# Thirty small loads on SyncE and six early stores on ScalarE in a decode kernel (1 core)

## The chip, the cores and the metric

The kernel runs on one core of a Trainium2 chip. Its metric is the device time of one execution in microseconds (us); smaller is better. A core has engines that run their own instruction streams side by side: TensorE (PE, matrix products), VectorE (DVE), ScalarE (ACT), GpSimd (POOL) and SyncE (SP), which here does nothing but issue transfers. They wait for one another through semaphores. Transfers between the chip's memory and the core's own memory are carried by 16 DMA engines; SyncE and ScalarE each issue into a queue of their own.

## The reference

One token for each of B = 2 batch rows goes through attention over a cache and through an MLP, and a gate mixes the two:

```
g = sigmoid((x * gate_w).sum(-1))                       # x: 2 x 1 x 1024
q = x @ wq                                              # 32 heads of 128
p = softmax(q . k_cache / sqrt(128))                    # k_cache: 2 x 32 x 16384 x 128, bf16
a = (p . v_cache) @ wo
x1 = x + shifted(gelu(layernorm(x) @ w1)) @ w2          # one position: the shifts leave zeros
b = x1 + gelu(layernorm(x1) @ w3) @ w4                  # F = 3584
out = g * a + (1 - g) * b                               # 2 x 1 x 1024, bf16
```

The two caches are 268 MB each and are read once. Everything else is small. Since the sequence has one position, the shifted input of the w2 product is zero, and the kernel does not load w1.

## The kernel before, in words

The kernel is first written down as a plan: `_Plan` holds for each engine a list of operations in order, each with its waits. `pl.add` appends an instruction, `pl.dma` appends a transfer on an engine's queue and returns the event "it has landed". The lists are then emitted engine by engine. An engine runs its list strictly in order: an operation whose wait isn't met holds up all that stand behind it.

Big loads go through a ring of five slots of 32 KB per partition. `queue_load` puts them into one list, in the order wq (two halves), w2, w3 (two halves), w4 (two halves), then for each of 32 pairs of heads the K load and the V load, and last wo (two halves, the second of them cut into five pieces). `pump` issues the head of that list on SyncE as soon as the plan has released its slots, with a wait for the release; `release` is called by the stage that has read a slot last. A K or V load fills two slots: 128 rows of 64 KB, 8.39 MB. K goes to slots 3 and 4 or 2 and 3 in turn (`k_slots`), V always to 0 and 1. So K of pair n+1 is issued when the first half of the scores of pair n is done, and V of pair n+1 when the value products of pair n are done. The names K0, K1, V3 and so on below count pairs from 0.

Ahead of the pairs stand the stages of `pro_stages`: the gate, the product with w2, the norm, the product with w3, the gelu (`gelu_stage`, whose tanh on ScalarE is L448 and whose result GT_bf on VectorE is L450), the product with w4 and the row bgrow (`st_bg`). ScalarE issues six small loads at the start: x and gate_w (L560, L561) and four pieces of x into `xrow` (L563), which `st_bg` adds.

For each pair n: `do_T` transposes K in place on VectorE (L647), `do_S` forms the scores on TensorE (L653), `do_softmax` takes the maximum, lets ScalarE do the exponential (L674) and transposes its result, `do_PV` multiplies with V on TensorE (L689), and `do_out` copies the sums on ScalarE (L698) and stores the two heads' column on VectorE (L703). The pairs are a hardware loop on TensorE, VectorE and ScalarE, two pairs to a turn; SyncE's list is unrolled. At the end `do_aproj` multiplies with wo (L726), VectorE copies the result (L750), and SyncE and ScalarE store one batch row each (L752).

Of the kernel before, what the change touches and what calls it, by code (L numbers as in the profile page):

```python
# [9 lines left out]
BF16 = mybir.dt.bfloat16  # L10
# [110 lines left out]
def build_kernel(nc, A_x, A_k, A_v, A_wq, A_wo, B_w1, B_w2, B_w3, B_w4, gate_w, out, dbg=None):  # L121
    dbg = dbg or {}
    B, Sq, D = A_x.shape
# [4 lines left out]
    P = 128  # L128
# [32 lines left out]
    PR = 32 * (NQ - 1) + 2  # L161
    assert DQ <= 512

    with ExitStack() as st:
        block = st.enter_context(nc.Block())
        sb = lambda name, shape, dt: st.enter_context(nc.sbuf_tensor(name, shape, dt))
# [34 lines left out]
        xrow = sb("xrow", [P, DQ], BF16)  # L201
        bgrow = sb("bgrow", [P, DQ], F32)
        orow = sb("orow", [P, DQ], BF16)
        m24 = sb("m24", [P, 2, NQ], F32)
        m2 = sb("m2", [P, 2], F32)
        gm = sb("gm", [P, 2], F32)
# [16 lines left out]
        sem = lambda n: st.enter_context(nc.semaphore(n))  # L223
        esems = {e: sem("e_" + e) for e in ENGS}
        s_ring = [sem(f"dr{i}") for i in range(NRS)]
        s_misc = sem("dmisc")
        s_gw = sem("dgw")
        s_out = [sem(f"dout{i}") for i in range(2)]
        s_xr = sem("dxr")
        s_tail = [sem(f"dtl{i}") for i in range(len(wo_runs[1]))]  # L230
        pl = _Plan(esems)
# [38 lines left out]
        for hp in range(HP):  # L270
# [7 lines left out]
                    waits=(ev_rowm,), sig=True)  # L278
# [3 lines left out]
        ev_cab = pl.add("dve", lambda e: e.tensor_scalar(cAB[:, 1:2], rowv[:, :], -NEG_BIG, NEG_BIG, op0=ALU.mult, op1=ALU.add),  # L282
                        waits=(e0,), sig=True)

        dma_q = []
        dma_done = {}
        slot_of = {}
# [12 lines left out]
        def pump():  # L300
            while dma_q and all(i in slot_free for i in dma_q[0][2]):
                key, fns, slots = dma_q.pop(0)
                waits = sum((slot_free.pop(i) for i in slots), ())
                slot_of[key] = slots[0]
                slots_of[key] = slots
                for k, fn in enumerate(fns):
                    dsem = s_ring[slots[0]] if len(fns) == 1 else s_tail[k]
                    dma_done[key] = dma_done[key, k] = pl.dma("sp", (lambda e, fn=fn, idx=slots[0]: fn(e, idx)), dsem,
                                                              waits=waits if k == 0 else ())

        def release(key, ev, slots=None):
            for idx in slots or slots_of[key]:
                assert idx not in slot_free
                slot_free[idx] = tuple(ev) if isinstance(ev, (tuple, list)) else (ev,)
            pump()
# [51 lines left out]
        evd = {}  # L367
# [176 lines left out]
        key = ("w2", 0)  # L544
        put([row_stage(key, list(range(NBD)), 0, NBD, lambda kc: shT_bf[:, kc, :], "const", last=True), hs_columns], key)
        put([st_x1, ln_a(x1T_f[:, :, :], "x1", st2_ps, "xn2"), ln_b(st2_ps, "xn2", None)])
        for hi in range(2):
            key = ("w3", hi)
# [3 lines left out]
        for hi in range(2):  # L552
            key = ("w4", hi)
# [8 lines left out]
        for qd in range(NQ):  # L562
            ev_xr = pl.dma("act", lambda e, qd=qd: e.dma_start(xrow[32 * qd:32 * qd + 2, :], A_x[:, 0, qd * DQ:(qd + 1) * DQ]), s_xr,  # L563
                           waits=(ev_xr0,))
# [8 lines left out]
        for pi in range(2):  # L573
            queue_load(("wo", pi), wloads[("wo", pi)], ((4, 3)[pi],))
        pump()

        def xcols(row, b_n, nb):
# [4 lines left out]
        for nb in range(NBD):  # L582
            last = pl.add("pe", lambda e, nb=nb: e.transpose(tr_ps[:, nb * 4:nb * 4 + 3], xcols(xg_row, 3, nb), ident[0:3, 0:3]),
                          waits=(ev_x, ev_gw, ev_ident), sig=(nb == NBD - 1))
# [10 lines left out]
        for hi in range(2):  # L595
            key = ("wq", hi)
            ev_arr = arrived(key)
            wv = ring_w(slot_of[key], RQ, HD)
            for r in range(RQ):
                kc = hi * RQ + r  # L600
                for h in range(H):
                    lastmm = (h == H - 1)
                    def fn(e, h=h, r=r, kc=kc, wv=wv, first=first):
                        return e.matmul(q_ps[:, h, :], lhsT=wv[:, r, h * Dh:(h + 1) * Dh], rhs=xT_bf[:, kc, :],  # L604
                                        start=first, stop=(kc == NBD - 1), skip_group_check=True)
# [6 lines left out]
        for bp in range(NBP):  # L612
            evp = pl.add("pe", lambda e, bp=bp: e.matmul(q4_ps[:, bp, :], lhsT=PermQ[:, bp, :],
                                                        rhs=q_sb[:, :, :].rearrange("p h b -> p (h b)"), start=True, stop=True),
                         waits=(ev_q, ev_const, ev_r0), sig=(bp == NBP - 1))
# [15 lines left out]
        def do_Z(n):  # L631
            g0 = (n // B * HP) * B + n % B
            for hp in range(HP):
                ev = pl.add("pool", lambda e, hp=hp: e.tensor_tensor(  # L634
                    Z[:, :, ZO:ZO + P].rearrange("p t (i c) -> p t i c", c=32)[:, :, 2 * hp:2 * hp + 2, hp],
                    q4_f[:, :, g0 + hp * B:g0 + hp * B + 1].broadcast_to([P, NBP, 2]),
                    mask4[:, 2 * hp:2 * hp + 2].unsqueeze(1).broadcast_to([P, NBP, 2]), op=ALU.mult),
                    waits=(ev_q4, ev_const, ev_S.get(n - 1)), sig=(hp == HP - 1))
            return ev
# [5 lines left out]
        def do_T(n, u):  # L645
            ap = chunk(n, u, TC).bitcast(F32)
            return pl.add("dve", lambda e: e.transpose(ap, ap), waits=(arrived(("k", n)),), sig=True)  # L647

        def do_S(n, u, w, first, last):
            kv = chunk(n, u, 1).rearrange("p (j b k t) -> p j b k t", j=JU, b=2, k=32)  # L650
            end = u % UH == UH - 1
            for bp in range(NBP):
                ev = pl.add("pe", lambda e, bp=bp: e.matmul(  # L653
                    S_ps[:, 0:NCOL], lhsT=Z[:, bp, ZO - 2 * u:ZO - 2 * u + P], rhs=kv[:, :, bp // 2, :, bp % 2],
                    start=(first and bp == 0), stop=(last and bp == NBP - 1), skip_group_check=True),
                    waits=w, sig=(end and bp == NBP - 1))
                w = ()
            if end:
                ev_S[n] = ev
                release(("k", n), ev, (slots_of["k", n][u // UH],))  # L660
# [22 lines left out]
        def do_PV(n, ev_pt):  # L683
            s0 = slot_of[("v", n)]
            vv = ring[:, s0:s0 + 2, :].rearrange("p s (u j d) -> p (s u) j d", u=UH, j=JU)
            w = (ev_pt, arrived(("v", n)))
            for jj in range(JU):
                for cg in range(4):
                    ev = pl.add("pe", lambda e, jj=jj, cg=cg: e.matmul(  # L689
                        acc_ps[32 * cg:32 * cg + 32, 0:512], lhsT=PT_sb[:, 32 * jj:32 * jj + 32], rhs=vv[:, 4 * cg:4 * cg + 4, jj, :],  # L690
                        start=(jj == 0), stop=(jj == JU - 1), tile_position=(0, 32 * cg), skip_group_check=True), waits=w,
                        sig=(jj == JU - 1 and cg == 3))
                    w = ()
            release(("v", n), ev)
            return ev

        def do_out(n, ev_pv, ev_rc):
            e1 = pl.add("act", lambda e: e.activation(acc_sb[:, :], acc_ps[:, 0:512], ACT.Copy), waits=(ev_pv,), sig=True)  # L698
            for w in range(4):
                e2 = pl.add("pe", lambda e, w=w: e.matmul(oT_ps, lhsT=acc_sb[:, w * P:(w + 1) * P], rhs=dsel[:, w, :],  # L700
                                                          start=(w == 0), stop=(w == 3)), waits=(e1,) if w == 0 else (), sig=(w == 3))
            b = n % B
            return pl.add("dve", lambda e, i: e.scalar_tensor_tensor(  # L703
                OT_sb[:, bass.ds(i * B * HP + b * HP, HP)], oT_ps, gT[:, b:b + 1], recip[:, :], op0=ALU.mult, op1=ALU.mult),
                waits=(e2, ev_rc), sig=True, dyn=True)
# [26 lines left out]

        for run in pro_stages:
            run()
        for n in range(NPR):
            pl.mark[n] = {e: len(pl.ops[e]) for e in ENGS}
            ev_z = do_Z(n)
            us = [h * UH + v for h in k_order[n % 2] for v in range(UH)]
            for k in range(0, NU, TC):
                ev_t = do_T(n, us[k])  # L740
                for t in range(TC):
                    w = () if t else (ev_t,) if k else (ev_t, ev_z) + pro_ev
                    do_S(n, us[k + t], w, k + t == 0, k + t == NU - 1)
            ev_pt, ev_rc = do_softmax(n)
            ev_OT = do_out(n, do_PV(n, ev_pt), ev_rc)
# [2 lines left out]

        ev_alast = do_aproj()
        ev_fin = pl.add("dve", lambda e: e.tensor_copy(orow[0:PR, :], rows_ps[0:PR, 0:DQ]), waits=(ev_alast,), sig=True)  # L750
        for b, eng in enumerate(("sp", "act")):
            ev_out = pl.dma(eng, lambda e, b=b: e.dma_start(out[b, 0, :].rearrange("(q n) -> q n", q=NQ), orow[b:PR:32, :]), s_out[b],  # L752
                            waits=(ev_fin,))
            pl.add(eng, lambda e, ev=ev_out: e.wait_ge(ev.sem, ev.val))
# [27 lines left out]
def bass_gated_mix__mha_block_cached__mixer_s_mlp__decode_kernel(  # L782
    nc: bass.Bass,
    A_x: bass.AP,
    A_k_cache: bass.AP,
    A_v_cache: bass.AP,
    A_wq: bass.AP,
    A_wo: bass.AP,
    B_x: bass.AP,
    B_w1: bass.AP,  # L790
    B_w2: bass.AP,
    B_w3: bass.AP,
    B_w4: bass.AP,
    gate_w: bass.AP,
    out: bass.AP,
):
    build_kernel(nc, A_x, A_k_cache, A_v_cache, A_wq, A_wo, B_w1, B_w2, B_w3, B_w4, gate_w, out)
# [28 lines left out]
```

## Time and profile before

| What | Value |
|---|---|
| time, median of 3 runs | 1326.04 us (1326.04 to 1326.1) |
| the profiled execution's own time | 1325.93 us |
| its span, first to last instruction | 1324.1 us |
| mean granted TensorE clock | 0.789 |
| read from memory | 570.44 MB, 431 GB/s over the span |
| TensorE busy | 785.1 us (59%) |
| VectorE busy | 657.2 us (50%) |
| ScalarE busy | 45.7 us (3%) |

How to read it: times in the traces are us from the start of the span, single durations of instructions often ns. L653 is line 653 of the kernel. In the order of time a row gives start, duration, engine, line, operation, what it writes and reads, and in brackets how long the engine idled before and what ended that. PE is the product, PEld the loading of its weights; SPq and ACTq are the transfers that SyncE and ScalarE issue. In the answers on DMA queues, q1 is SyncE's queue and q10 ScalarE's; q8 and q14 carry the program itself. A line there gives packets, MB and the time that the packets took as a share of all 16 DMA engines over the window. A line of the stretches gives their length, then busy time and count for PE, PEld, DVE, ACT and POOL, the granted clock, the DMA share and GB/s.

### The profile page before, as it was taken

The page shows a single profiled execution, that of the slowest core. Times are in us where ns is not written, and L with a number is a line of the kernel's source. Part 1 is how long each engine was busy: PE and PEld are TensorE (multiplying, and loading weights), DVE is VectorE, ACT ScalarE, POOL GpSimd, SP SyncE. Part 2 cuts the span into 40 slices and gives each one's busy share as a digit, 9 for nine tenths or more (in the row PEclk, how much of TensorE's full clock was granted, in tenths as well). Part 3 has the DMA queues.
Part 4 walks back from the last instruction along what each step waited for, and adds up shares of the span by engine and source line. Part 5 has one row for each costly group of instructions (what it writes and reads, how often), then busy time and mean ns, then how long its engine had stood idle before and what let it go on. Part 6 is the DMA issues. An engine that isn't in the chain of part 4 may idle for free.

```text
span 1324.1 us, 12290 instructions
## 1 busy us (share of the span) xinstructions
PE 785.1 (59%) x5235; PEld 335.8 (25%) x5235; DVE 657.2 (50%) x523; ACT 45.7 (3%) x99; POOL 23.5 (2%) x110
## 2 busy tenths in 40 slices
PE   3645557656556765555676555566655456665646
PEld 2512223222222322222232222222222222222223
DVE  1054446655444665544466554446655444665543
ACT  0000000000000000000000000000000000000000
POOL 3000000000000000000000000000000000000000
PEclk9966787777678777767877776788787788878679
DMA  9999999999999999999999999999999999999998
GB/s 403 445 424 434 436 434 434 432 438 432 430 440 432 430 440 430 430 440 430 434 436 430 438 434 436 432 432 438 434 428 440 432 430 440 430 432 438 430 434 359
DMA packets 11138, 570.60 MB, mean 431 GB/s; under 512 B 1252, under 2 KB 1268, under 8 KB 1655
## 3 DMA queue, kind: packets, MB, share of 16 engines
q1 hardware_dynamic: 11096, 570.43, 99.7%
q8 instruction: 8, 0.13, 0.0%
q10 hardware_dynamic: 30, 0.01, 0.0%
q14 instruction: 4, 0.02, 0.0%
HBM read 570.44 MB, written 0.00 MB: 431 GB/s over the span
## 4 chain that ended last, share of the span: by engine, by line
DMA 70%; PE 23%; DVE 6%; issue 0%; SPq 0%
DMA ring<-in_A_k_cache_dram 65%; PE ps L653 23%; DVE ring L647 6%; DMA ring<-in_B_w_dram 3%; DMA ring<-in_A_wo_dram 2%; PE ps L466 1%; SPq L324 0%; DVE orow L750 0%; PE ps L726 0%
## 5 line engine op out<-in xcount | busy, mean ns | idle before, releaser
L653 PE MATMUL ps<-ring,Z 128*128 128x512 bf16 x2048 | 534.5, 420 | 389.1 <-DVE ring L647 388.5
L647 DVE STREAM_TRANSPOSE ring<-ring 128x2048 f32<-128x2048 f32 x256 | 565.2, 2275 | 278.6 <-DMA ring<-in_A_k_cache_dram 278.6
L653 PEld LDWEIGHTS ps<-ring,Z 128*128 128x128 bf16 x2048 | 204.4, 104 | 706.7 <-issue 473.5
L689 PE MATMUL ps<-ring,PT_sb 128*32 128x512 bf16 x2048 | 168.2, 501 | 4.1 <-DVE recip L680 3.7
L703 DVE SCALAR_TENSOR_TENSOR OT_sb<-ps,gT,recip 128x2 f32 x32 | 7.0, 220 | 203.4 <-PE ps L700 203.4
L689 PEld LDWEIGHTS ps<-ring,PT_sb 128*32 128x32 bf16 x2048 | 67.6, 122 | 90.8 <-issue 69.6
L674 ACT ACTIVATE P_sb<-ps,negm 128x512 bf16<-128x512 f32 x32 | 22.0, 687 | 1013.9 <-DVE negm L672 1013.9
L663 DVE TENSOR_REDUCE rA<-ps 128x1 f32<-128x512 f32 x32 | 22.1, 692 | 64.1 <-PE ps L653 64.1
L678 PE MATMUL ps<-rowsum,hsel 128*128 128x1 f32 x128 | 24.0, 291 | 37.9 <-ACT P_sb L674 37.9
L676 DVE STREAM_TRANSPOSE PT_sb<-P_sb 128x512 bf16<-128x512 bf16 x32 | 22.8, 711 | 27.0 <-ACT P_sb L674 27.0
L634 POOL TENSOR_TENSOR Z<-q_f,mask 128x8 bf16<-128x8 f32 x64 | 12.3, 227 | 1214.3 <-PE ps L653 1214.3
L678 PEld LDWEIGHTS ps<-rowsum,hsel 128*128 128x128 f32 x128 | 21.3, 236 | 40.7 <-ACT P_sb L674 40.7
L665 PE MATMUL ps<-ident,rmax_bf 128*1 128x128 bf16 x32 | 6.9, 217 | 33.1 <-DVE rmax_bf L664 33.1
L698 ACT ACTIVATE acc_sb<-ps 128x512 bf16<-128x512 f32 x32 | 19.1, 597 | 198.8 <-PE ps L689 198.8
L700 PE MATMUL ps<-dsel,acc_sb 128*128 128x2 bf16 x128 | 8.1, 167 | 22.5 <-ACT acc_sb L698 22.5
L466 PE MATMUL ps<-xn_bf,ring 128*128 128x2 bf16 x224 | 14.5, 202 | 2.9 <-DMA ring<-in_B_w_dram 2.9
L466 PEld LDWEIGHTS ps<-xn_bf,ring 128*128 128x128 bf16 x224 | 14.4, 172 | 3.0 <-DMA ring<-in_B_w_dram 3.0
L700 PEld LDWEIGHTS ps<-dsel,acc_sb 128*128 128x128 bf16 x128 | 5.3, 96 | 38.2 <-ACT acc_sb L698 38.2
L665 PEld LDWEIGHTS ps<-ident,rmax_bf 128*1 128x1 bf16 x32 | 2.5, 79 | 48.9 <-DVE rmax_bf L664 48.9
L604 PE MATMUL ps<-xT_bf,ring 128*128 128x2 bf16 x256 | 7.1, 165 | 11.7 <-DVE xT_f L588 7.4
L666 DVE TENSOR_REDUCE m_sb<-ps 1x2 bf16<-1x128 bf16 x32 | 8.9, 278 | 9.9 <-PE ps L665 9.9
L672 DVE TENSOR_SCALAR negm<-ps,cAB 128x1 f32<-128x1 f32 x32 | 8.9, 277 | 9.2 <-PE ps L669 9.2
(97 smaller groups left out, 85.8 us busy)
## 6 DMA issues: line engine op xcount, KB each, us to landing
ring<-in_B_w_dram SPq DMA_DIRECT2D x4, 3584.0 KB, 35.4
ring<-in_A_wq_dram SPq DMA_DIRECT2D x2, 4096.0 KB, 17.5
ring<-in_A_wo_dram SPq DMA_DIRECT2D x1, 4096.0 KB, 40.2
ring<-in_B_w_dram SPq DMA_DIRECT2D x1, 2048.0 KB, 27.1
ring<-in_A_wo_dram SPq DMA_DIRECT2D x1, 2048.0 KB, 22.2
ring<-in_A_wo_dram SPq DMA_DIRECT2D x1, 1024.0 KB, 24.4
ring<-in_A_k_cache_dram SPq DMA_DIRECT2D x32, 26.8
ring<-in_A_v_cache_dram SPq DMA_DIRECT2D x32, 29.2
```

What stands on the lines that cost most here:

```text
L466: fn = lambda e, nb=nb, kl=kl: e.matmul(out_ps[:, nb, :], lhsT=cols(wv, kl, nb, nout), rhs=rhs_of(k0 + kl), start=False, stop=True, skip_g ...
L634: ev = pl.add("pool", lambda e, hp=hp: e.tensor_tensor(Z[:, :, ZO:ZO + P].rearrange("p t (i c) -> p t i c", c=32)[:, :, 2 * hp:2 * hp + 2, ...
L647: return pl.add("dve", lambda e: e.transpose(ap, ap), waits=(arrived(("k", n)),), sig=True)
L653: ev = pl.add("pe", lambda e, bp=bp: e.matmul(S_ps[:, 0:NCOL], lhsT=Z[:, bp, ZO - 2 * u:ZO - 2 * u + P], rhs=kv[:, :, bp // 2, :, bp % 2], ...
L663: e1 = pl.add("dve", lambda e: e.tensor_reduce(rA[:, :], S_ps[:, 0:NCOL], axis=AX.X, op=ALU.max), waits=(ev_S[n],), sig=True)
L665: e3 = pl.add("pe", lambda e: e.transpose(mt_ps, rmax_bf[:, :], ident[:, :]), waits=(e2,), sig=True)
L674: e7 = pl.add("act", lambda e: e.activation(P_sb[:, :], S_ps[:, 0:NCOL], ACT.Exp, bias=negm[:, 0:1], scale=scale, accum_out=rowsum[:, 0:1] ...
L676: e8 = pl.add("dve", lambda e: e.transpose(PT_sb[:, :], P_sb[:, :]), waits=(e7,), sig=True)
L678: e9 = pl.add("pe", lambda e, hp=hp: e.matmul(l_ps[:, hp:hp + 1], lhsT=hsel[:, hp, :], rhs=rowsum[:, 0:1], start=True, stop=True, skip_gro ...
L689: ev = pl.add("pe", lambda e, jj=jj, cg=cg: e.matmul(acc_ps[32 * cg:32 * cg + 32, 0:512], lhsT=PT_sb[:, 32 * jj:32 * jj + 32], rhs=vv[:, 4 ...
L698: e1 = pl.add("act", lambda e: e.activation(acc_sb[:, :], acc_ps[:, 0:512], ACT.Copy), waits=(ev_pv,), sig=True)
L700: e2 = pl.add("pe", lambda e, w=w: e.matmul(oT_ps, lhsT=acc_sb[:, w * P:(w + 1) * P], rhs=dsel[:, w, :], start=(w == 0), stop=(w == 3)), w ...
```

## The change

A tile `marks` of 16 partitions is added, which nothing reads, and two semaphores. In `pump`, right behind the issue of V0 and again right behind that of V3, SyncE also issues fifteen loads from gate_w into it: load m (1 to 15) has m rows of 4m elements (8m bytes). SyncE waits for all of them once, at the end, ahead of the output store.

Between the prologue's stages and the first pair, ScalarE issues six stores from `xrow` into the output: two of 4 rows (512 B each), two of 16 rows (128 B), two of 32 rows (128 B); of each shape one takes neighbouring partitions and the other takes partitions at a step. The first waits for the gelu's result GT (L450), each further one for the landing of the one before, and after the sixth ScalarE waits for its landing. SyncE waits for the sixth again at the end, ahead of the output store. What they write to the output is overwritten there by the result.

```diff
+        marks = sb("marks", [16, 2, 16, 128], BF16)
...
+        mark_at = (("v", 0), ("v", 3))
         dma_q = []
         dma_done = {}
         slot_of = {}
...
                     dsem = s_ring[slots[0]] if len(fns) == 1 else s_tail[k]
                     dma_done[key] = dma_done[key, k] = pl.dma("sp", (lambda e, fn=fn, idx=slots[0]: fn(e, idx)), dsem,
                                                               waits=waits if k == 0 else ())
+                if key in mark_at:
+                    mi = mark_at.index(key)
+                    for m in range(1, 16):
+                        dma_done["marks"] = pl.dma("sp", lambda e, m=m, mi=mi: e.dma_start(
+                            marks[0:m, mi, m, 0:4 * m], gate_w[0:4 * m * m].rearrange("(k c) -> k c", k=m)), s_marks)
...
         for run in pro_stages:
             run()
+        o1 = out[1, 0, :]
+        early = [lambda e: e.dma_start(o1.rearrange("(q n) -> q n", q=4), xrow[0:4, :]),
+                 lambda e: e.dma_start(o1.rearrange("(q n) -> q n", q=4), xrow[1:PR:32, :]),
+                 lambda e: e.dma_start(o1.rearrange("(q n) -> q n", q=16), xrow[0:16, 0:D // 16]),
+                 lambda e: e.dma_start(o1.rearrange("(q n) -> q n", q=16), xrow[0:P:8, 0:D // 16]),
+                 lambda e: e.dma_start(out.rearrange("b s (q n) -> (b s q) n", q=16), xrow[0:32, 0:D // 16]),
+                 lambda e: e.dma_start(out.rearrange("b s (q n) -> (b s q) n", q=16), xrow[0:P:4, 0:D // 16])]
+        ev_early = evd["GT"]
+        for fn in early:
+            ev_early = pl.dma("act", fn, s_early, waits=(ev_early, ev_xr))
+        pl.add("act", lambda e: e.wait_ge(ev_early.sem, ev_early.val))
         for n in range(NPR):
...
         ev_fin = pl.add("dve", lambda e: e.tensor_copy(orow[0:PR, :], rows_ps[0:PR, 0:DQ]), waits=(ev_alast,), sig=True)
+        pl.add("sp", lambda e: e.wait_ge(dma_done["marks"].sem, dma_done["marks"].val))
+        pl.add("sp", lambda e: e.wait_ge(ev_early.sem, ev_early.val))
```

More of the change, by code (lines that the diff above doesn't have):

```diff
@@ L226, in build_kernel @@
         s_misc = sem("dmisc")
+        s_marks = sem("dmarks")
+        s_early = sem("dearly")
         s_gw = sem("dgw")
```

## The prediction

> **What bounds the kernel now.** I read the page first, then the grouped stretches, then the chain that ended last, then the order of time of SyncE and ScalarE. The page:
>
> ```profile
> span 1324.1 us, 12290 instructions
> PE 785.1 (59%) x5235; PEld 335.8 (25%) x5235; DVE 657.2 (50%) x523; ACT 45.7 (3%) x99; POOL 23.5 (2%) x110
> ...
> DMA  9999999999999999999999999999999999999998
> ...
> q1 hardware_dynamic: 11096, 570.43, 99.7%
> q8 instruction: 8, 0.13, 0.0%
> q10 hardware_dynamic: 30, 0.01, 0.0%
> ```
>
> No compute engine is above 59%. SyncE's queue (q1) keeps all 16 DMA engines busy 99.7% of the span: the kernel is a stream of 570 MB and ends when the slowest DMA engine has moved its share. One pair of loads (8.39 MB of K, 8.39 MB of V) in the stretches by window:
>
> ```profile
> 121.08:159.79 38.71, 23.37 (x139) 9.58 (x139) 20.18 (x15) 1.38 (x3) 0.38 (x2) 0.76 1.00 434
> ```
>
> 38.71 us, DMA share 1.00, 434 GB/s. One engine moves 16 rows of 64 KB in that time, so a 64 KB row takes it 38.71/16 = 2.42 us. A w4 row (28 KB) takes 1.06 us by the same rate, a wq row (32 KB) 1.21 us, and one load of K or V 19.35 us. I call the time of one row a turn.
>
> So there are two ways to lose time: put more packets on an engine, or issue a load so late that the queue runs empty. How much slack the second has is in the chain and in SyncE's own issues:
>
> ```profile
> 53.33 29.03 DMA ring<-in_A_k_cache_dram
> ...
> 94.89 26.17 DMA ring<-in_A_k_cache_dram
> 121.08 2.32 DVE ring L647
> 123.52 9.49 PE ps L653 x32
> 133.02 26.75 DMA ring<-in_A_k_cache_dram
> ```
>
> ```profile
> 66.27 0.33 SPq L353 DMA_DIRECT2D ring<-in_A_v_cache_dram  x1
> 94.89 0.33 SPq L349 DMA_DIRECT2D ring<-in_A_k_cache_dram  x1
> 112.24 0.33 SPq L353 DMA_DIRECT2D ring<-in_A_v_cache_dram  x1
> ...
> 188.44 0.33 SPq L353 DMA_DIRECT2D ring<-in_A_v_cache_dram  x1
> 210.98 0.33 SPq L349 DMA_DIRECT2D ring<-in_A_k_cache_dram  x1
> ```
>
> K1 is issued at 94.89 and lands at 121.06. V1 is issued at 112.24, only 8.8 us before the engines would have nothing left. That issue is what the change can touch, through ScalarE:
>
> ```profile
> 54.54 0.25 ACT L448 ACTIVATE gl_a<-gl_b 128x56 f32<-128x56 f32 x1 [24.44 <-DVE gl_b L447]
> 104.19 0.69 ACT L674 ACTIVATE P_sb<-ps,negm 128x512 bf16<-128x512 f32 x1 [49.40 <-DVE negm L672]
> ...
> 112.25 0.60 ACT L698 ACTIVATE acc_sb<-ps 128x512 bf16<-128x512 f32 x1 [7.28 <-PE ps L689]
> ```
>
> ```profile
> 55.05 0.22 DVE L450 TENSOR_TENSOR GT_bf<-gl_b,gl_x 128x56 bf16<-128x56 f32 x1
> ```
>
> ScalarE idles from 54.8 to 104.19. Then comes the first exponential, the PV products wait for it, and the end of PV frees the slots for V1: V1 is issued 8.05 us after the exponential starts.
>
> **Part 1: the thirty loads on SyncE.** Issue: the four xrow loads below take 1.15 us, 0.29 each, so a set takes 4.3 us. After V0 that is 66.60 to 70.9 with the next issue at 94.89; after V3 it is 188.77 to 193.1 with the next at 210.98. Both hide in SyncE's waiting for slots; without that cover it would be 4.3 us a set. Engine time: the 30 packets of ScalarE's queue fit one packet per row plus one closing packet per engine used (2+2, 1+1, four times 2+2, 4+4). So I read a load of m rows as m engines with a row and a closing packet each: 240 packets a set, 30 of them on the engine that takes part in all fifteen. Price from the output's own stores at the end and, from above, the 2 KB rows of the last wo loads; first ScalarE's issue, then the windows 1323.1 to 1323.4 and 1319 to 1320:
>
> ```profile
> 1321.89 0.60 ACTq L752 DMA_DIRECT2D out_dram<-orow  x1
> ```
>
> ```profile
> q10 hardware_dynamic: 8, 0.00, 2.9%
> ```
>
> ```profile
> DMA packets 144, 0.26 MB, mean 262 GB/s; under 512 B 20, under 2 KB 20, under 8 KB 144
> ...
> q1 hardware_dynamic: 144, 0.26, 68.2%
> ```
>
> 2.9% of 16 x 0.3 us over 8 packets is 17 ns each (512 B rows and closings); 68.2% of 16 us over 144 is 76 ns each. The added rows have 8 to 120 B, nearest the first: 30 x 17 ns = 0.5 us a set on the fullest engine, 1.0 us for both. Bounds: 0 (if that engine is not the slowest) and 60 x 76 ns = 4.5 us. The Trainium skill, "DMA: Bandwidth & Descriptors", section Specifications, says that below 512 B a DMA engine does a read-modify-write; no run here shows such a row, and by that rule the price would lie nearer the upper bound. The unread tile has no reader, and SyncE's two added waits at the end lie in 25.8 us of idling:
>
> ```profile
> SPq L752 <- DVE orow L750: 25.8, 1, 25.8
> ```
>
> **Part 2: the six stores on ScalarE.** Each waits for the one before to have landed, and a seventh wait ends the chain; behind it in ScalarE's order stands the exponential. The chain starts at 55.27, when GT is written. What a small transfer takes beside the big loads shows in the xrow loads, issued beside 32 KB rows. ScalarE's issue; then the window 15.2 to 19.4 (no packet under 8 KB, so none of these yet), 15.2 to 19.85, and 20.1 to 25.1:
>
> ```profile
> 15.22 1.15 ACTq L563 DMA_DIRECT2D xrow<-in_A_x_dram  x4
> ```
>
> ```profile
> DMA packets 52, 1.68 MB, mean 400 GB/s; under 512 B 0, under 2 KB 0, under 8 KB 0
> ```
>
> ```profile
> q10 hardware_dynamic: 2, 0.00, 0.1%
> ```
>
> ```profile
> q10 hardware_dynamic: 14, 0.00, 0.3%
> ```
>
> The first row on each of two engines starts 4.2 to 4.6 us after the issue; the other 14 packets follow over about five microseconds, seven behind each first one: roughly one turn of the big stream (1.21 us, later 0.6 for the 16 KB rows of w2) per small packet. The Trainium skill, same page, section Queues, rings and completion order, says that an engine alternates between queues by packets of typically 9 to 17 descriptors. The trace disagrees: a wq load gives an engine 8 rows, 9.7 us, and the small rows did not wait that long. By the rule, with 8 rows as a packet, each of a store's two or three turns would last 19.35 us (rival c).
>
> At the idle end a store's packets run within 1.2 to 1.5 us of its issue (1321.89 to the window above); I take 1.3. The remaining 3.1 us of the xrow loads can be read in two ways. As time (work already on the engine, whatever its rows): a store beside 64 KB rows needs 4.4 for its first row, about 1.8 more because turns are longer and the slowest of 4 or 16 engines counts, 2.42 for the closing packet, 0.4 until ScalarE goes on (my estimate; the page's span leaves 0.7 after the last packets): 9.0. As turns (2.5 of them): 1.3 + 2.5 x 2.42 + about 1.2 for the slowest engine + 2.42 + 0.4 = 11.4. The two stores with 32 rows have two rows per engine, one turn more: 11.4 or 13.8. The first store runs beside w4 rows: 4.4 + 1.06 + 0.4 = 5.9, done at 61.2. Three stores and two long ones more: 61.2 + 3 x 9.0 + 2 x 11.4 = 111.0, or 61.2 + 3 x 11.4 + 2 x 13.8 = 123.0. About half of that is phase I can't know, and near 101 the small loads of part 1 shorten some turns, so I take the point between: ScalarE free at 116, with 111 and 123 as ends. The packets themselves are at most 14 per engine, 0.2 us.
>
> The exponential then starts 116 - 104.19 = 11.8 us late and V1 is issued at 124.1, after K1 has landed. What a load needs from an empty queue:
>
> ```profile
> DMA to landing us min/median/max: 12.2/27.5/43.2
> ```
>
> The 12.2 is the first wq load, 4.19 MB, 9.66 us at 434 GB/s: 2.5 us of lead, against 1.3 for the small store; I take 2.0. V1 lands at 124.1 + 2.0 + 19.35 = 145.4 instead of 121.06 + 19.35 = 140.4: 5.0 us lost. In general the loss is (ScalarE free) - 111.0, never below 0. Nothing wins it back, since the engines are full from there on; nor does it repeat: S1 would start about 4 us late, K2 is then issued near 137, 8 us ahead of V1's landing.
>
> **Sum.** 5.0 for the stall; the first set of small loads then falls into it (0), the second adds 0.5: 5.5. The profiled execution took 1325.93 us (span 1324.1 and 1.8 around it), 0.1 under the median of 1326.04. 1325.93 + 5.5 = 1331.4; I say 1331.
>
> **The rivals.** (a) The stores stay hidden: if only about one turn of 64 KB is ahead of a store's first row (1.3 + 1.2 + 2.42 + 0.4, some 5.5 us, three-turn stores 8), ScalarE is free near 94 to 105 and V1 is on time. For it: the wait may be bound to the kind of the transfer, since the xrow loads read memory beside a full stream while the stores read the core's own. Against: a store is queued behind the same big rows. What is left is 1.0 us of packets: 1327. It decides at ScalarE free before 111. (b) The chain is much longer: the closing packet of a store waits for its write into memory under load, or rows under 512 B are slow. Then 3 us more on each of six stores end at 134: 23 us lost, 1349. Against it: at the idle end the output's packets lie within 0.3 us of each other. (c) An engine finishes all 8 rows of a K or V load before it turns to ScalarE's queue, so that a turn is 19.35 us: five stores beside K and V take 5 x 2 x 19.35 = 193 us and the second rows 39 more; ScalarE is free after 250 and some 140 us are lost: 1466. Against it stand the xrow windows. (It is what the rule of the Trainium skill's page "DMA: Bandwidth & Descriptors", cited above, would give.) (d) Faster: nothing here takes work away; a few tenths at most by another phase between the engines.
>
> **How the numbers follow.** A change under 0.2% (2.7 us) is about what a measurement of this kernel can't tell from none. Forecast (ScalarE free between 111 and 123, loss up to 12 plus small packets): 0.58, of which 0.06 lie in its low end within 0.2%. (a) 0.28, all within 0.2% but 0.02 above it for dear small packets. (b) 0.10, (c) 0.02, (d) 0.02 faster. So faster 0.02, same 0.28 + 0.06 - 0.02 = 0.32, slower 0.66. The forecast's own range is 1327 to 1338. The range for 8 in 10 reaches down through (a) to 1326.3 and up to 1338: what lies outside is (b), (c), most of (d) and a little of (a).
>
> **What would show it.** In the changed profile: ScalarE's early stores issued 9 to 12 us apart beside K and V; the first exponential near 116 instead of 104.19; V1's issue near 124; one slice with less than 430 GB/s about 125 us; 480 more packets on q1 and 176 on q10; after that every K and V 38.7 us apart as before. Wrong it is if the exponential still starts at 104 to 107 (rival a), or if the small loads move K1's landing by more than 1 us (their price is mis-sized), or if stores are 20 us and more apart.

## The result and the profile after

| Kernel | Median | Runs | Ratio to before |
|---|---|---|---|
| before | 1326.03 us (1325.84 to 1326.1) | 8 | |
| changed | 1329.16 us (1328.63 to 1331.1) | 8 | 1.0026, 95% interval 1.0015 to 1.0037 |

The change costs 3.1 us. The time lies 1.8 us under the forecast of 1331 and inside its range, but the profile tells another story than the sum: the stall that was to carry 5 of 5.5 us does not appear in the profiled execution. That execution took 1328.63 us, the fastest of the eight; note also that the runs, within 0.3 us of each other before, now spread over 2.5 us. One run of the kernel with rows of 1 KB, further down, took 1388 us at a granted clock of 0.57 in place of 0.78 to 0.80 and is left out of its median.

The page of the changed kernel: its span, SyncE's queue (480 packets more, as counted) and ScalarE's (176 more).

```profile
span 1326.8 us, 12328 instructions
...
q1 hardware_dynamic: 11576, 570.45, 99.6%
...
q10 hardware_dynamic: 206, 0.03, 0.0%
```

ScalarE's order of time in the changed kernel (start, duration, engine, line):

```profile
55.17 0.27 ACTq L745 DMA_DIRECT2D out_dram<-xrow  x1
60.74 0.60 ACTq L746 DMA_DIRECT2D out_dram<-xrow  x1
69.15 0.34 ACTq L747 DMA_DIRECT2D out_dram<-xrow  x1
78.38 0.56 ACTq L748 DMA_DIRECT2D out_dram<-xrow  x1
87.14 0.32 ACTq L749 DMA_DIRECT2D out_dram<-xrow  x1
98.14 0.52 ACTq L750 DMA_DIRECT2D out_dram<-xrow  x1
110.78 0.69 ACT L683 ACTIVATE P_sb<-ps,negm 128x512 bf16<-128x512 f32 x1 [56.12 <-DMA out_dram<-xrow]
```

The chain of stores is there, one store every 8.4 to 9.2 us and 11.0 and 12.6 for those with 32 rows, and the exponential waits for its end: the row names the store as what released it, where it named VectorE before. But it waits until 110.78, not 116. SyncE's issues and the chain that ended last:

```profile
66.55 5.72 SPq L317 DMA_DIRECT2D marks<-in_gate_w_dram  x15
93.66 0.36 SPq L358 DMA_DIRECT2D ring<-in_A_k_cache_dram  x1
117.75 0.35 SPq L362 DMA_DIRECT2D ring<-in_A_v_cache_dram  x1
```

```profile
93.66 28.34 DMA ring<-in_A_k_cache_dram
...
134.00 26.71 DMA ring<-in_A_k_cache_dram
...
172.13 27.29 DMA ring<-in_A_k_cache_dram
...
211.95 27.72 DMA ring<-in_A_k_cache_dram
```

And two lines of the same view of the kernel before, for K3 and K4, which the prediction did not need:

```profile
171.16 27.30 DMA ring<-in_A_k_cache_dram
...
210.98 26.19 DMA ring<-in_A_k_cache_dram
```

Start plus duration is the landing: K1 at 122.00 (before 121.06), K2 at 160.71 (159.77), K3 at 199.42 (198.46), K4 at 239.67 (237.17). K1 is late by 0.94 us, K2 and K3 by 0.94 and 0.96, K4 by 2.5. The two steps stand right behind V0 and behind V3, where the small loads are. V1 was issued at 117.75, 5.5 us late, and yet K2's lateness is no larger than K1's: in this execution the late V1 cost nothing that shows.

### The profile page after: what moved, and what is told of

Same layout as the page of the kernel before. It is cut to its first block, busy times and chain, and to the rows that moved or that the text cites. A ratio compares the mean times of both kernels' runs of the same rounds, so it can differ in the third digit from the quotient of the medians.

```text
span 1326.8 us, 12328 instructions
## 1 busy us (share of the span) xinstructions
PE 788.1 (59%) x5235; PEld 335.1 (25%) x5235; DVE 657.0 (50%) x523; ACT 45.7 (3%) x99; POOL 23.5 (2%) x110
## 4 chain that ended last, share of the span: by engine, by line
DMA 71%; PE 23%; DVE 6%; issue 0%; SPq 0%
DMA ring<-in_A_k_cache_dram 66%; PE ps L662 22%; DVE ring L656 6%; DMA ring<-in_B_w_dram 3%; DMA ring<-in_A_wo_dram 2%; PE ps L475 1%; SPq L333 0%; DVE orow L770 0%; PE ps L735 0%
## 5 line engine op out<-in xcount | busy, mean ns | idle before, releaser
L662 PEld LDWEIGHTS ps<-ring,Z 128*128 128x128 bf16 x2048 | 201.4, 104 | 700.8 <-issue 455.7
L698 PE MATMUL ps<-ring,PT_sb 128*32 128x512 bf16 x2048 | 173.8, 514 | 4.3 <-DVE recip L689 4.3
```

Source lines behind the costliest of these rows:

```text
L662: ev = pl.add("pe", lambda e, bp=bp: e.matmul(S_ps[:, 0:NCOL], lhsT=Z[:, bp, ZO - 2 * u:ZO - 2 * u + P], rhs=kv[:, :, bp // 2, :, bp % 2], ...
L698: ev = pl.add("pe", lambda e, jj=jj, cg=cg: e.matmul(acc_ps[32 * cg:32 * cg + 32, 0:512], lhsT=PT_sb[:, 32 * jj:32 * jj + 32], rhs=vv[:, 4 ...
```

## Two theories and how they were told apart

Theory A, formed from this profile: the small loads themselves hold up the engines by 1.0 and 1.5 us, and the stores are hidden. Theory B is the prediction's: the stores' chain empties the queue, and the small loads are cheap. The first four kernels take the two parts apart. Each expectation below calls them A and B.

**Only the loads** (stores and their waits removed).

```diff
-        ev_early = evd["GT"]
-        for fn in early:
-            ev_early = pl.dma("act", fn, s_early, waits=(ev_early, ev_xr))
-        pl.add("act", lambda e: e.wait_ge(ev_early.sem, ev_early.val))
```

> Only the two sets of small loads on SyncE; the six stores and their waits are gone. Theory A (the small loads themselves hold up the DMA engines, and the stores are hidden): in the changed kernel K1 landed 0.95 us later than before and K4 2.48 us later, so about +2.6 us, 1328.6, and the runs lie close together. Theory B (the prediction's: the chain of stores delays V1 and empties the queue, the small loads cost 17 ns a packet): +1.0 us at most, 1327.

Measured: 1328.56 us (1328.4 to 1328.97, 11 runs) against 1326.00, ratio 1.0019 (1.001 to 1.0028): +2.56 us, in a narrow spread. A's number, and two and a half times B's.

**Only the stores** (the loop over `mark_at` in `pump` and SyncE's wait for it removed).

```diff
-                if key in mark_at:
-                    mi = mark_at.index(key)
-                    for m in range(1, 16):
-                        dma_done["marks"] = pl.dma("sp", lambda e, m=m, mi=mi: e.dma_start(
-                            marks[0:m, mi, m, 0:4 * m], gate_w[0:4 * m * m].rearrange("(k c) -> k c", k=m)), s_marks)
```

> Only the six stores and ScalarE's waits; no small loads. Theory A: ScalarE is free near 111 to 113 and V1 is issued near 118 to 120, about when the slowest DMA engine runs dry (121.06 less 1.1 to 2 us): 1326.0 to 1327, and runs whose chain is longer lose a little more, so the runs are spread. Theory B: most of the cost is here, +2 to +5 us, 1328 to 1331.

Measured: 1327.93 us (1326.1 to 1329.13, 11 runs), ratio 1.0013 (1.0004 to 1.0022): +1.9 us. So A is wrong here: the stores aren't hidden as a rule. B's mechanism is there, and its size varies: two of the eleven runs lost 0.1 us, one 3.1. In the profiled execution (1327.93 us) the exponential, V1's issue, and K1 and K2 in the chain:

```profile
111.28 0.69 ACT L678 ACTIVATE P_sb<-ps,negm 128x512 bf16<-128x512 f32 x1 [56.50 <-DMA out_dram<-xrow]
```

```profile
119.04 0.33 SPq L357 DMA_DIRECT2D ring<-in_A_v_cache_dram  x1
```

```profile
94.72 26.33 DMA ring<-in_A_k_cache_dram
...
132.87 28.42 DMA ring<-in_A_k_cache_dram
```

K1 lands at 121.05, on time. K2 lands at 161.29 instead of 159.77: V1, issued at 119.04, came too late to follow K1 without a break, and 1.5 us are gone between the two. The trace also records every single packet with its start, duration and size. By these records no engine starts a row of V1 before 120.0, and the first V1 rows take 2.5 to 3.3 us where nearly all other 64 KB rows take 2.42.

**A longer chain** (the fourth store done twice, seven in all, no loads).

```diff
+                 lambda e: e.dma_start(o1.rearrange("(q n) -> q n", q=16), xrow[0:P:8, 0:D // 16]),
```

> As the run with the stores alone, with the fourth store (16 rows) done twice, which adds one step of the chain of 8.8 us (87.14 - 78.38 in the changed kernel). Both theories agree that ScalarE is then free near 120 to 122 and V1 is issued near 128: the queue runs empty. By the prediction's sum (ScalarE free less 111) 9 to 11 us are lost, 1335 to 1337; if the lead of a load from an empty queue is nearer 1.3 than 2.0 us, 0.7 less. If the stores can't stall the stream at all: 1326.

Measured: 1336.88 us (1336.34 to 1338.02, 4 runs), ratio 1.0085 (1.0069 to 1.01): +10.9 us. The profiled execution (1336.34):

```profile
119.59 0.69 ACT L678 ACTIVATE P_sb<-ps,negm 128x512 bf16<-128x512 f32 x1 [64.85 <-DMA out_dram<-xrow]
```

```profile
127.30 0.33 SPq L357 DMA_DIRECT2D ring<-in_A_v_cache_dram  x1
```

```profile
140.72 28.73 DMA ring<-in_A_k_cache_dram
```

K2 lands at 169.45, 9.7 late. With six stores ScalarE was free at 111.28 for 1.5 us lost, with seven at 119.59 for 9.7: 8.3 us later, 8.2 us more. The loss is (ScalarE free) less 109.8 to 109.9, one for one. The prediction had this line with 111.0. Counted from V1's issue, K2 lands 42.25 us later with six stores (161.29 - 119.04) and 42.15 with seven (169.45 - 127.30). That is 3.4 to 3.5 us more than two loads take in the full stream (38.71), and it is what a load that comes too late loses between its issue and the full pace.

**Five stores** (the sixth removed, no loads).

```diff
-                 lambda e: e.dma_start(out.rearrange("b s (q n) -> (b s q) n", q=16), xrow[0:P:4, 0:D // 16])]
```

> Stores alone, without the sixth; no small loads. In the run with all six ScalarE issued the sixth at 99.17, so it is free near 99, ahead of the exponential's 104. If the stores cost only through ScalarE being late: 1326.0 and the runs within 0.3 us of each other, as before. If the writes themselves disturb the stream: some five sixths of the 1.9 us, 1327.6.

Measured: 1326.07 us (1325.94 to 1326.24, 10 runs) against 1325.96, ratio 1.0001 (0.9991 to 1.0011). The exponential is back at its old place:

```profile
104.33 0.69 ACT L678 ACTIVATE P_sb<-ps,negm 128x512 bf16<-128x512 f32 x1 [49.52 <-DVE negm L676]
```

The median is 0.1 us above the kernel before, which the interval does not tell from nothing: if the writes themselves disturb the stream, it is too little to see here. What six and seven stores cost is accounted for by ScalarE's lateness, and the spread goes with it: five are well clear of the edge, seven are far beyond it, six stand on it.

## What the small loads cost

**One set** (behind V0 only, no stores).

```diff
-        mark_at = (("v", 0), ("v", 3))
+        mark_at = (("v", 0),)
```

> Only the first set of small loads (behind V0), no stores. Theory A: about +1.0 us, 1327.0, K1 landing 0.9 to 1.1 us late and everything behind it late by the same. Theory B: +0.5 us at most.

Measured: 1327.18 us (1327.14 to 1327.25, 10 runs), ratio 1.0009 (1.0 to 1.0018): +1.2 us. With +2.56 for both, the second set costs 1.4. In the profiled execution K1 lands at 122.00, 0.94 late, as in the changed kernel:

```profile
93.26 28.74 DMA ring<-in_A_k_cache_dram
```

Spread over the 30 packets of the fullest engine, 1.2 us is 40 ns a packet where the prediction took 17. The next kernels vary the run of small packets.

**Two sets in a row behind V0.**

```diff
-                    mi = mark_at.index(key)
-                    for m in range(1, 16):
+                    for mi in range(2):
+                        for m in range(1, 16):
```

> No stores; behind V0 the set of small loads twice over (30 loads, up to 60 packets on an engine), none behind V3. One set cost 1.2 us. If the price goes by the packet: 2.4 us, 1328.4. If what costs is one gap behind the burst (the engine has read nothing of the next big row ahead), the gap is there once: 1.2 us plus 30 packets of about 10 ns, 1327.2 to 1327.6.

Measured: 1329.39 us (1329.14 to 1330.05, 8 runs) against 1325.96, ratio 1.0026 (1.0015 to 1.0037): +3.4 us, more than either reading: not once the gap, and not twice the price but three times.

**One load of 120 rows.**

```diff
-                    for m in range(1, 16):
-                        dma_done["marks"] = pl.dma("sp", lambda e, m=m, mi=mi: e.dma_start(
-                            marks[0:m, mi, m, 0:4 * m], gate_w[0:4 * m * m].rearrange("(k c) -> k c", k=m)), s_marks)
+                    dma_done["marks"] = pl.dma("sp", lambda e: e.dma_start(
+                        marks[0:120, :], gate_w[0:960].rearrange("(k c) -> k c", k=120)), s_marks)
```

> No stores; behind V0 one load of 120 rows of 16 B instead of the fifteen loads of 1 to 15 rows (also 120 rows), so each engine that takes part gets 8 rows and one closing packet instead of up to 30 packets. If the price goes by the load (fifteen closings and issues): 0.1 us, 1326.1. If by the row or by a gap that any burst leaves: 0.3 to 1.2 us, 1326.3 to 1327.2.

**Loads 1 to 8 alone.**

```diff
-                    for m in range(1, 16):
+                    for m in range(1, 9):
```

> No stores; behind V0 only loads 1 to 8 (36 rows, up to 16 packets on an engine). By the packet: 16/30 of 1.2 us, 1326.6. One gap of a fixed size behind any burst: 1.2 us, 1327.2.

Measured: 1326.28 us (1326.13 to 1326.43, 10 runs; ratio 1.0002, 0.9992 to 1.0012) for the one load and 1326.16 (1326.05 to 1326.37, 10 runs; 1.0002, 0.9992 to 1.0011) for the eight, +0.3 and +0.2 us, neither told from nothing by its interval. K1 lands at 121.11 and 121.00 in their profiled executions, against 121.06 before: a short run of packets is nearly free.

**The same thirty loads, five at a time** (behind V0 to V5, no stores).

```diff
-        mark_at = (("v", 0), ("v", 3))
+        mark_at = tuple(("v", n) for n in range(6))
...
-                    mi = mark_at.index(key)
-                    for m in range(1, 16):
+                    mi, third = divmod(mark_at.index(key), 3)
+                    for m in range(5 * third + 1, 5 * third + 6):
```

> No stores; all thirty loads of both sets, but five at a time behind V0 to V5 (loads 1 to 5, 6 to 10, 11 to 15, twice), so at most 10 packets stand in a row on an engine. So far a run of 9 or 16 packets cost 0.2 to 0.3 us, of 30 1.2, of 60 3.4. If only what goes beyond some 14 packets in a row costs (75 ns each, from (3.43 - 1.18)/30): the 2.6 us of the two whole sets shrink to a few tenths, 1326.1 to 1326.5. If every packet costs the same wherever it stands: 1328.5. If each burst has a price of its own of 0.2 to 0.3 us: 1327.2 to 1327.8.

Measured: 1327.06 us (1326.88 to 1327.48, 10 runs) against 1325.98, ratio 1.0008 (0.9999 to 1.0018): +1.1 us instead of 2.6. The interval just reaches down to no loss, but all ten runs lie above every run of the kernel before (1326.16 at most). The first two readings miss the number: it is not a few tenths, and not the full price. The third, a price for each burst, has the sum about right (0.18 us each) but not the bursts. K1 to K6 land -0.09, -0.03, 0.26, 0.25, 0.52 and 0.80 us later than before, K6 by this line (315.37, before 314.57):

```profile
287.74 27.63 DMA ring<-in_A_k_cache_dram
```

So loads 1 to 5 cost nothing either time, loads 6 to 10 cost 0.06 and 0.27 us, loads 11 to 15 0.29 and 0.28. The packet records below say why.

**Larger rows** (one set behind V0; rows of 512 B from w2 as in the diff, and of 1 KB with 512 in place of 256).

```diff
-        marks = sb("marks", [16, 2, 16, 128], BF16)
+        marks = sb("marks", [16, 1, 16, 256], BF16)
...
-                            marks[0:m, mi, m, 0:4 * m], gate_w[0:4 * m * m].rearrange("(k c) -> k c", k=m)), s_marks)
+                            marks[0:m, mi, m, :], B_w2[0:m, 0:256]), s_marks)
```

> As the run with one set of loads, but every row has 512 B (taken from w2, of the same unread tile's size) instead of 8 to 120 B. If the price of the set (1.2 us) comes from the rows being under 512 B: it falls to 30 packets of 17 ns, 0.5 us, 1326.5. If it comes from the number of packets in a row that find nothing of the next big row read ahead: about the same as before, 1.2 us and at most 15 x 15 ns more, 1327.1 to 1327.4.

> The same with rows of 1 KB (an engine moves one in about 40 ns, from 76 ns for 2 KB). If the added bytes only fill time that the engine stands still anyway: 1.2 to 1.4 us, 1327.1 to 1327.4. If bytes and packets add up: 1.2 + 15 x 0.04 = 1.8 us, 1327.8.

Measured: 1327.31 us (1327.14 to 1327.38, 10 runs) for 512 B, ratio 1.001 (1.0 to 1.0019), +1.4 us; 1328.08 us (1327.54 to 1328.28, 9 runs) for 1 KB, ratio 1.0015 (1.0005 to 1.0025), +2.2 us, against 1325.92. Rows of 512 B aren't cheaper than rows under 512 B: the read-modify-write of the Trainium skill ("DMA: Bandwidth & Descriptors", section Specifications) is not what the set costs. By the packet records the rows under 512 B took 8 to 13 ns each, those of 512 B 25 to 64. The rows of 1 KB add 1.0 us to the one set's 1.2, so bytes don't hide in the gap either; that is more than the 0.6 us that they were expected to take.

Where the time goes is in the packet records. They don't name the engine, but an engine's packets follow one another without a gap, and the sizes tell the loads apart: load m puts one row of 8m bytes on each of m engines. So the first engine gets 30 packets of a set (15 rows, 15 closing packets), the second 28, and so on down to 2; the sixteenth gets none. In the changed kernel, behind V0:

| Packets of the set in a row on an engine | K1's first 64 KB row behind them, us |
|---|---|
| 2 to 10 | 2.42 |
| 12 | 2.53 |
| 14 | 2.85 |
| 16 | 3.32 |
| 20 | 3.63 |
| 24 | 3.72 |
| 30 | 4.22 |

The small packets themselves are cheap: a run of 30 is through in 0.20 us, a run of 20 in 0.15. What costs is the big row behind them: here it keeps its 2.42 us behind up to 10 packets, and takes 0.9 us more behind 16, 1.2 behind 20 and 1.8 behind 30. In the run with the loads alone these rows differ from the table by at most 0.07 us. With loads 1 to 8 the row behind 16 packets took 3.09 us, with the one load of 120 rows (9 packets) none took more than 2.47, and with two sets in a row some took 6.26. In the run with one set a few runs of packets were slower (26 in 1.33 us) and the row behind them shorter (2.69). All engines of the table see the same fifteen loads issued, so what counts is how many packets the engine itself gets. Whether its rows or its closing packets do it isn't told apart, since each load brings one of both.

The records also show which engine decides. The engines don't run level: before the change five of them start K1's first row at 100.8 to 101.3, the other eleven at 99.3 to 100.1, and K1 has landed when the last one is done. In the changed kernel the last one is the sixth engine, with 20 packets. Its first K1 row ends at 104.63; before the change the last engine's ended at 103.71. That is 0.92 us, and K1 is late by 0.94. The first engine, with 30 packets, loses more but ends this row at 104.27, because it was about 1 us ahead. Loads 1 to 8 put only 6 packets on the sixth engine, and K1 isn't late. Loads 1 to 5 put none there, loads 6 to 10 and 11 to 15 put 10 there, which is the pattern of the split loads; the rows behind 10 packets took 2.5 to 2.7 us behind V1. With two sets in a row the last first row ends at 106.77, 3.06 late, and K1 lands 3.02 late.

So the price of a set isn't the fullest engine's. It is what the run of packets does to the engine that is last, and engines that are ahead use up their lead first.

## The change arranged to cost less

All its transfers, the loads five at a time as above, the sixth store and ScalarE's wait behind the last pair.

```diff
-        for fn in early:
+        for fn in early[:5]:
             ev_early = pl.dma("act", fn, s_early, waits=(ev_early, ev_xr))
-        pl.add("act", lambda e: e.wait_ge(ev_early.sem, ev_early.val))
...
         assert not dma_q, "unissued DMAs remain"
+        ev_early = pl.dma("act", early[5], s_early, waits=(ev_early, ev_xr))
+        pl.add("act", lambda e: e.wait_ge(ev_early.sem, ev_early.val))
```

> All transfers of the change, placed elsewhere: the loads five at a time behind V0 to V5, the first five stores as they were, the sixth store and ScalarE's wait for it behind the last pair instead of ahead of the first. If the two causes are all there is (long runs of small packets; ScalarE late for the first exponential): 1326.1 to 1326.6. If the transfers cost wherever they stand: 1328 to 1329.

Measured: 1327.17 us (1327.0 to 1327.38, 11 runs), ratio to before 1.0009 (1.0 to 1.0018), a miss by 0.6 us and for the reason of the split loads. Against those alone (1327.06) the six stores add 0.1 us. It is 2 us better than the change and its runs are close together again; it isn't better than the kernel before, which has less to do.

## Why the prediction was right, and where not

- **The bound** held: the stream of big loads fills the engines, and what is lost isn't won back. K1 to K3 keep a lateness of 0.94 to 0.96 us, and K31 is still late by 2.56 (1284.66 against 1282.10).
- **Counting** held: 480 and 176 packets. SyncE's issue took 5.7 and 5.3 us a set instead of 4.3 and lay in its waiting as said.
- **The price of the small loads** was mis-sized: "30 x 17 ns = 0.5 us a set on the fullest engine" stands against 1.2 and 1.4 measured. The sum priced the packets' own time, which was even less (30 packets in 0.20 us), and put the big row behind them at nothing; that row took up to 1.8 us longer. Nor did the fullest engine decide, but the sixth, with 20 packets. The upper bound of 4.5 us held, by the price of 2 KB rows and not by what happened. The prediction's own sign for a mis-sized price, K1's landing moved by more than 1 us, was just not reached in the changed kernel (0.94) and was met with the loads alone (1.48).
- **The stores' chain**: the reading "as time" gave 9.0 and 11.4 us a store and 111.0 for its end; measured 8.4 to 9.2, 11.0 and 12.6, and 110.78. The packet records bear out its parts: for the third store the rows start 3.5 to 6.3 us after the issue (4.4 + 1.8 in the prediction), each closing packet 2.43 behind its row, and ScalarE goes on 0.5 after the last of them. The reading "as turns" (11.4, 13.8, 123.0) is refuted. The step that failed is "I take the point between": 116 was the middle of two mechanisms, and neither of them gives it.
- **From ScalarE's lateness to the loss**: the one-for-one line held, with 109.8 in place of 111.0. The term that was too small is the lead of a load from an empty queue: "I take 2.0" stands against 3.4 to 3.5 measured, more than the 2.5 that the first wq load showed. With V1's issue 7.7 us after the exponential (8.05 in the prediction) that gives 121.06 - 3.5 - 7.7 = 109.9. The late end of the chain and the short lead went opposite ways: a stall of 5.0 us was forecast, and the stores alone lose 1.9 in the median.
- **The overlap** held in that the two losses don't add up, but the other way round than "the first set of small loads then falls into it (0)". Apart the two parts cost 2.56 and 1.93, together 3.1 instead of 4.5. In the profiled execution it is the stall that falls into the first set: with K1 late by 0.94, the last moment for V1's issue moves from about 117.6 to about 118.5 (K1's landing less 3.5), and V1 was issued at 117.75. There the late V1 cost nothing beside the late K1. How much of the stall is left in the slower runs was not profiled.
- **Rivals**: (a) hidden stores is what the fastest runs of the stores alone show, but not the median. By the mark that the prediction set for it, ScalarE free before 111, the profiled execution (110.78) lies on its side, but not by its mechanism: the stores took 8.4 us and more, not 5.5, and its 1327 has the loads too cheap as well. (b) and (c) did not occur: a chained store took 8.4 to 12.6 us, not 19 and more a turn. Their prices were too high in any case. While ScalarE holds V1 back, SyncE has nothing else to issue, so behind K1's landing near 121 the rest of a longer chain would have run beside no big rows (this follows from the kernel's order; it was not run). And the terms of (c), 61 + 193 + 39, end at 293, not at 250.

So the sum came out near (5.5 against 3.1) with a stall too large and loads too small. That these two errors offset each other, and that the time fell into the range with most of the cost on the loads, is luck.

## What to carry to other kernels

In a kernel whose DMA engines are always full, ask two things of any added transfer: how many packets stand in a row on each DMA engine, above all on the one that is last, and whose wait for its landing holds up an engine that later frees a slot. In this kernel small transfers in groups of up to 10 packets on an engine cost 0.3 us at most for a group, and the stores cost nothing that could be seen as long as ScalarE was free in time. Where two mechanisms give two ends, forecast one of them and keep the other as a rival; and a wait that ends near the edge of the slack shows as spread between runs before it shows as time.

## What the runs showed of the hardware that was not expected

- Small packets in a row on an engine cost little themselves (30 in 0.20 us), but the 64 KB row behind them takes longer: 2.4 to 2.7 us behind 10, 3.1 to 3.4 behind 16, 3.6 behind 20, 4.2 behind 30, up to 6.3 in the run with up to 60. Rows of 512 B instead of 8 to 120 B are no cheaper (1.4 us a set against 1.2). The first rows of V1 behind a break in the stream take longer too (2.5 to 3.3 us). That an engine normally starts to fetch the next big row while it moves the one before, and can't do so across a long run of small packets or a break, would fit both; no run shows it, and why the rows take longer stays open.
- The DMA engines don't run level: five of them start K1 0.7 to 2.0 us behind the others before the change, the same number run behind in the changed kernel, and a load lands with the last one. An engine that is ahead can lose that much unseen.
- A small store beside 64 KB rows took 7.8 to 9.7 us from its issue to the next one's, over all profiles with stores, and 10.7 to 12.6 with two rows to an engine; beside 28 KB rows 5.6 to 6.4. An engine puts one 64 KB row between a store's row and its closing packet (2.43 us). At the idle end a store's packets were through within 1.5 us.
